# Six zero products in front of the fifth pair's first burst: attention and a gated MLP on one Trainium2 core

## The chip, the core and the metric

The kernel runs on one core of a Trainium2 chip. The core has engines that work side by side: TensorE (PE in the rows, with its weight loads as PEld), VectorE (DVE), ScalarE (ACT), GpSimd (POOL), and SyncE (SP), which issues most of the DMAs. Each engine takes its instructions in the order of the program and waits on semaphores for the others. The metric is the device time of one execution in microseconds (us).

## What is computed

```python
# attention: batch 4, 8 heads, 576 positions, head size 64
q_rot, k_rot = rotate(q), rotate(k)
scores = q_rot @ k_rot.T / sqrt(64)
attn = softmax(scores)
x = (attn @ v) -> [2304, 512]
# gated MLP: 512 -> 2048 -> 512
h = x @ w_in
out = (h * sigmoid(1.702 * h)) @ w_out
```

All inputs and the output are float32.

## The kernel before

The 32 heads are worked as 16 pairs; a pair's two heads share the 128 partitions. For a pair, `prep` loads q, k and v, rotates q and k, and turns them on PE against an identity (line 525) into the operands of the scores. `scores` (line 650) multiplies them into PSUM slots of the pool SPS, DVE negates and takes the minimum (line 681), ACT takes the exponential (line 684), and the result stands in the tile TP.

The first four pairs turn TP on PE and multiply it by whole blocks of v (lines 795 to 833). From the fifth pair on, `weighted` does it otherwise: DVE transposes TP in small blocks (line 689), v lies in the tile VR, four times over on 32 partitions each, and PE multiplies 32 keys at a time (line 756). The 18 groups of keys are done in two parts, here called bursts. A burst has 72 float32 products; PE does each in two passes, and the trace shows the 144 passes as 144 products and as many weight loads. Both bursts gather in two slots of SPS, from which ACT and DVE copy the pair's result into XS (lines 384 and 386).

Between the fifth pair's two bursts stands a turn of four blocks for a later pair (line 525, RAW_102). It writes the slot PT_67, which DVE has to read out first (line 536, pieces of the tile KL).

The MLP runs on chunks of 256 tokens between the pairs: `moe` multiplies x with w_in (line 939), then with w_out (line 956). Weights come through OW (line 890) and are split on ACT, DVE and POOL (lines 894 to 906, tile CW).

Nothing is scheduled on the chip: every operation has a number in the order in which the program creates it, the table `PLACES` gives each number its place in one global order, `ENGINES` gives it an engine where there is a choice, and each engine's queue is that order with the other engines' work left out. SP's queue is ordered so too: a DMA that waits holds up those behind it.

Near the start, 30 float32 products of a tile that DVE has set to zero (T's first slot, line 438) run on PE (line 443). Nothing reads their result:

```python
    zeros = op(DVE, 140.0, f, prio=-1e6)
    warm = plan.buf("SPS", (2,))
    for i in range(at["n_warm"]):
        pe(lambda: nc.tensor.matmul(warm.t[:, 0, 0:128], plan.tiles["T"][0][:, 0:128], plan.tiles["T"][0][:, 0:128],
                                    start=True, stop=True), zeros, f32=[128], bufs=[warm], prio=1e9)
```

Of the kernel before, what the change touches and what calls it, by code (L numbers as in the profile page):

```python
# [326 lines left out]
def attention_moe(ctx: ExitStack, tc: tile.TileContext, q, k, v, w_in, w_out, cos_sin, out):  # L327
    nc = tc.nc
# [21 lines left out]
                 A=([128, 2, CT], F32), U=([128, CT], F32))  # L350
# [91 lines left out]
    for i in range(at["n_warm"]):  # L442
        pe(lambda: nc.tensor.matmul(warm.t[:, 0, 0:128], plan.tiles["T"][0][:, 0:128], plan.tiles["T"][0][:, 0:128],  # L443
                                    start=True, stop=True), zeros, f32=[128], bufs=[warm], prio=1e9)
# [804 lines left out]
```

## Time and profile before

| | before |
|---|---|
| median of 3 runs | 657.63 us (656.05 to 659.46) |
| profiled execution, its own time | 658.57 us |
| its span, first to last instruction | 656.9 us |
| PE busy | 627.8 us, 96% of the span |
| DVE, ACT, POOL busy | 76%, 52%, 42% |
| mean granted TensorE clock | 0.991 of full speed |
| DMA moved | 107.16 MB, 163 GB/s on average |

Busy time says how long an engine had at least one instruction at work; an engine that waits is idle. The chain of waits is followed back from the last instruction: at each step to what released it. A timeline row gives the start, the time that the merged instructions took, the engine, the line, what is written and read, the count, and in brackets the idle time before it and what ended it. "Issue" stands for time in which an engine waited for nothing that the profile shows. A window row gives each engine's busy time in a stretch with its count of instructions in brackets. PEclk is the clock that TensorE was granted, 1.00 for 2.4 GHz and 0.50 for 1.2 GHz.

### The profile page before, as it was taken

What the parts mean: (1) busy time and instruction counts of PE and PEld (TensorE: products, weight loads), DVE (VectorE), ACT (ScalarE), POOL (GpSimd) and SP (SyncE); (2) the same over time, 40 slices, a digit from 0 to 9 for tenths busy, and PEclk for the clock granted to TensorE, in tenths of its full rate; (3) what the DMA queues carried; (4) which work ended last, traced back from release to release, by engine and by line L of the source; (5) the groups of instructions that cost most, each with busy time, mean ns of one, the idle gap of its engine ahead of it and who ended that gap; (6) DMA issues with size and microseconds to landing.
All of it is one profiled execution on the core that took longest, in us unless ns stands there. A gap on an engine that the chain in (4) does not pass through costs nothing.

```text
span 656.9 us, 18242 instructions
## 1 busy us (share of the span) xinstructions
PE 627.8 (96%) x7258; PEld 524.9 (80%) x7258; DVE 501.1 (76%) x1133; ACT 341.5 (52%) x830; POOL 277.5 (42%) x309
## 2 busy tenths in 40 slices
PE   9999976899999998999999999999999999999997
PEld 7655554688778786888788888888999989898985
DVE  6999989699999998968889967866485456645352
ACT  3998985366668664536364643634143233233221
POOL 2643535152636373626561666651102343132321
PEclk9999998989999999999999999999999999999999
DMA  7654657797977878775465765653726523242401
GB/s 192 149 137 132 187 156 208 167 218 215 247 190 174 242 198 244 199 221 152 145 160 170 210 172 145 172 133 100 268 78 209 179 110 128 81 146 80 145 0 66
DMA packets 82994, 107.16 MB, mean 163 GB/s; under 512 B 41254, under 2 KB 60892, under 8 KB 79708
## 3 DMA queue, kind: packets, MB, share of 16 engines
q1 hardware_dynamic: 82764, 105.74, 57.1%
q8 instruction: 57, 0.93, 0.6%
q10 hardware_dynamic: 144, 0.25, 0.2%
q14 instruction: 29, 0.24, 0.1%
HBM read 71.68 MB, written 23.91 MB: 146 GB/s over the span
## 4 chain that ended last, share of the span: by engine, by line
PE 69%; DVE 14%; DMA 5%; ACT 4%; POOL 4%; issue 3%; SPq 1%; POOLq 0%; DVEq 0%; ACTq 0%
PE SPS L1128 14%; PE PT L939 12%; PE SPS L956 12%; PE SPS L650 7%; PE SPS L756 7%; PE SPS L1087 6%; PE PT L1087 6%; DVE TP L681 3%; DMA OW<-in_moe_w_out_dram 2%; DVE TP L689 2%; DVE CW L903 2%; PE SPS L443 1%; PE SPS L820 1%; PE PT L795 1%; DMA VR<-in_v_dram 1%
## 5 line engine op out<-in xcount | busy, mean ns | idle before, releaser
L939 PE MATMUL PT<-XC,win 128*128 128x256 f32 x960 | 134.6, 287 | 1.7 <-ACT G L384 1.6
L939 PEld LDWEIGHTS PT<-XC,win 128*128 128x128 f32 x960 | 124.1, 189 | 13.2 <-issue 7.9
L956 PE MATMUL SPS<-wout,G 128*128 128x512 f32 x480 | 131.1, 402 | 1.0 <-POOL G L387 0.4
L684 ACT ACTIVATE TP<-TP,ST 128x576 f32<-128x576 f32 x144 | 110.8, 771 | 28.3 <-DVE TP L681 28.0
L681 DVE TENSOR_SCALAR_CACHE_REDUCE TP<-SPS 128x576 f32<-128x576 f32 x144 | 103.7, 745 | 12.3 <-PE SPS L650 12.0
L956 PEld LDWEIGHTS SPS<-wout,G 128*128 128x128 f32 x480 | 83.8, 189 | 20.1 <-issue 3.4
L1128 PE MATMUL SPS<-wout,G 128*128 128x512 f32 x384 | 96.3, 394 | 0.0
L396 POOL TENSOR_TENSOR G<-T,G 128x256 fp32r<-128x256 f32 x68 | 50.1, 740 | 82.2 <-ACT G L384 38.7
L689 DVE STREAM_TRANSPOSE TP<-TP 128x576 f32<-128x576 f32 x108 | 78.9, 757 | 1.6 <-ACT TP L684 1.4
L1128 PEld LDWEIGHTS SPS<-wout,G 128*128 128x128 f32 x384 | 69.2, 188 | 13.2 <-ACT O L391 0.4
L906 POOL TENSOR_TENSOR CW<-CW 128x512 int32<-128x512 int32 x32 | 41.5, 1302 | 70.8 <-DVE CW L903 16.0
L756 PE MATMUL SPS<-TP,VR 32*64 32x144 f32 x3456 | 63.0, 292 | 6.5 <-DVE TP L689 3.9
L384 ACT CAST G<-T 128x256 fp32r<-128x256 f32 x89 | 35.9, 404 | 60.2 <-PE SPS L956 25.2
L756 PEld LDWEIGHTS SPS<-TP,VR 32*64 32x64 f32 x3456 | 55.9, 134 | 14.0 <-DVE TP L689 6.2
L387 POOL TENSOR_SCALAR G<-T 128x256 fp32r<-128x256 f32 x55 | 22.4, 409 | 97.2 <-DVE T L1119 27.4
L945 ACT ACTIVATE T<-PT 128x256 f32<-128x256 f32 x80 | 30.2, 379 | 42.1 <-PE PT L939 33.8
L1117 ACT ACTIVATE T<-U 128x256 f32<-128x256 f32 x64 | 25.5, 416 | 46.7 <-DVE U L396 37.8
L650 PE MATMUL SPS<-KH 64*128 64x288 f32 (+1 forms) x216 | 45.5, 341 | 4.1 <-DVE TP L681 3.1
L396 DVE TENSOR_TENSOR G<-T,G 128x256 fp32r<-128x256 f32 x76 | 33.6, 447 | 17.0 <-POOL G L387 10.9
L650 PEld LDWEIGHTS SPS<-KH 64*128 64x128 f32 (+1 forms) x216 | 25.9, 186 | 17.9 <-DVE TP L681 7.8
L650 PE MATMUL SPS<-KH,KL 64*128 64x288 f32 (+1 forms) x216 | 39.5, 300 | 0.0
L396 POOL TENSOR_TENSOR XS<-XS 128x576 fp32r<-128x576 f32 (+1 forms) x24 | 34.3, 1432 | 12.0 <-ACT XS L384 4.6
(131 smaller groups left out, 1105.4 us busy)
## 6 DMA issues: line engine op xcount, KB each, us to landing
TR<-t_dram SPq DMA_DIRECT2D x16, 1024.0 KB
VR<-VR SPq DMA_DIRECT2D x36, 288.0 KB
x_dram<-XS SPq DMA_DIRECT2D x16, 576.0 KB
XC<-x_dram SPq DMA_DIRECT2D x18, 512.0 KB
OW<-in_moe_w_in_dram SPq DMA_DIRECT2D x16, 512.0 KB
OW<-in_moe_w_out_dram SPq DMA_DIRECT2D x16, 512.0 KB
RQ<-in_k_dram SPq DMA_DIRECT2D x40, 142.0 KB
RQ<-in_q_dram SPq DMA_DIRECT2D x40, 142.0 KB
```

The costliest lines, as they stand in the source:

```text
L384: return nc.scalar.copy(to, src)
L396: return engine[e].tensor_tensor(to, a, b, op=how)
L650: nc.tensor.matmul(ss[h].t[:, c, 0:HALF], of[x][rows, S + t * 128:S + t * 128 + 128], of[y][rows, c * HALF:c * HALF + HALF], start=(m == 0 ...
L681: o = vec("DVE", "psum", S, lambda e: nc.vector.tensor_scalar(tile_to(), src(), by, LARGEST, op0=ALU.mult, op1=ALU.min, accum_out=st.t[:, ...
L684: o = vec("ACT", "sbuf", S, lambda e: nc.scalar.activation(to(), to(), AF.Exp, bias=st.t[:, 0, t:t + 1], scale=-1.0, accum_out=st.t[:, 1, ...
L689: return o, vec("DVE", "psum", S, lambda e: nc.vector.transpose(to(), to()), o, bufs=[tp], prio=prio + at["exp"] + at["across"])
L756: nc.tensor.matmul(bank[64 * h:64 * h + 64, 0:144], vr.t[rows, h, a], of()[rows, a, 144 * h:144 * h + 144], start=(a == 0), stop=(a == n_k ...
L906: o = vec("POOL", "two", DM, lambda e, a=a, r=r: nc.gpsimd.tensor_tensor(a().bitcast(I32), a().bitcast(I32), r(), op=ALU.add), o, low, buf ...
L939: nc.tensor.matmul(h.t[:, 0:CT], win[f_i // KH][:, wl, kk, f_i % KH * 128:(f_i % KH + 1) * 128], xc[xl].t[:, kk, :], start=(i == m == 0), ...
L956: nc.tensor.matmul(acc.t[:, m, :], g.t[:, a, m * 128:(m + 1) * 128], wout[f_i // KH][:, b, f_i % KH, :], start=(f_i == fs[0] and i == 0), ...
L1087: nc.tensor.matmul(h(to), w(a)[:, k], x(b)[:, k], start=(begin and n == 0), stop=(n == 5), skip_group_check=True)
L1128: nc.tensor.matmul(acc[j].t[:, m, :], g.t[:, x, m * 128:(m + 1) * 128], wout[f_i // KH][:, y, f_i % KH, :], start=(begin and n == 0), stop ...
```

## The change

Six more products of the zero tile, again into the third slot of SPS, are created behind the 30 of the warm-up. Nothing reads them.

```diff
+    fill = plan.buf("SPS", (2,))
+    for i in range(6):
+        pe(lambda: nc.tensor.matmul(fill.t[:, 0, 0:128], plan.tiles["T"][0][:, 0:128], plan.tiles["T"][0][:, 0:128],
+                                    start=True, stop=True), zeros, f32=[128], bufs=[fill], prio=1e9)
```

Since six operations are created, all later ones have a number that is six higher, and so the tables `PLACES` and `ENGINES` are written out anew. In `PLACES` the six get places just ahead of the fifth pair's first burst; the order of everything else is as before on every engine. The five added lines move all later line numbers by five (756 becomes 761).

The first place is PE's queue ahead of the fifth pair's first burst. SPS_64 to SPS_66 are the three score slots, PT_67 is a slot for turned blocks, RAW the rotated q and k, T_74 the zero tile. Before:

```order
L650 MATMUL SPS_64<-KL_92,KH_91 128x288
L525 MATMUL PT_67<-ident,RAW_101 128x128 x4
L525 MATMUL PT_67<-ident,RAW_103 128x128
L756 MATMUL SPS_65<-TP_96,VR_97 64x144 x2
L756 MATMUL SPS_64<-TP_96,VR_97 64x144 x2
```

and with the change:

```order
L655 MATMUL SPS_64<-KL_92,KH_91 128x288
L530 MATMUL PT_67<-ident,RAW_101 128x128 x4
L530 MATMUL PT_67<-ident,RAW_103 128x128
L448 MATMUL SPS_66<-T_74 128x128 x6
L761 MATMUL SPS_65<-TP_96,VR_97 64x144 x2
L761 MATMUL SPS_64<-TP_96,VR_97 64x144 x2
```

The six stand between the turn of a single block and the burst, and nothing else has moved.

The second place is the same, with what each instruction waits for:

```order
L530 MATMUL PT_67<-ident,RAW_103 128x128 [waits DMAHW3_49,DMAHW4_49,DVE_49,Pool_49]
L448 MATMUL SPS_66<-T_74 128x128 [waits Activation_49]
L448 MATMUL SPS_66<-T_74 128x128 x5
L761 MATMUL SPS_65<-TP_96,VR_97 64x144 [waits DVE_49]
L761 MATMUL SPS_65<-TP_96,VR_97 64x144 [waits DMAHW3_49]
```

The first of the six has a wait on ACT, the last reader of its slot; the burst's own waits, on DVE and on the v loads, are the ones that it had.

## Rows read from the trace of the kernel before

**Rows 1.** The page: engines' busy time; queue, kind: packets, MB, share of 16 engines.

```profile
PE 627.8 (96%) x7258; PEld 524.9 (80%) x7258; DVE 501.1 (76%) x1133; ACT 341.5 (52%) x830; POOL 277.5 (42%) x309
...
q8 instruction: 57, 0.93, 0.6%
```

**Rows 2.** Timeline of PE, 103 to 121 us: start, us, engine, line, operation [idle before].

```profile
104.78 0.60 PE L525 MATMUL PT<-ident,RAW 128*128 128x128 f32 x4
107.81 0.30 PE L525 MATMUL PT<-ident,RAW 128*128 128x128 f32 x1 [2.44 <-issue]
110.43 4.63 PE L756 MATMUL SPS<-TP,VR 32*64 32x144 f32 x144 [2.31 <-DVE TP L689]
115.19 0.86 PE L525 MATMUL PT<-ident,RAW 128*128 128x128 f32 x4
115.98 2.29 PE L756 MATMUL SPS<-TP,VR 32*64 32x144 f32 x129
120.40 0.50 PE L756 MATMUL SPS<-TP,VR 32*64 32x144 f32 x15 [2.13 <-issue]
```

**Rows 3.** The chain of waits: start, us, what.

```profile
122.99 5.43 DMA OW<-in_moe_w_out_dram
...
144.80 2.44 PE SPS L756 x144
```

**Rows 4.** Windows: stretch, length, PE, PEld, DVE, ACT, POOL busy, PEclk, DMA share, GB/s.

```profile
107.80:108.84 1.04, 0.30 (x1) 0.12 (x1) 1.04 (x2) 1.04 (x4) 1.04 (x2) 1.00 1.05 414
108.84:110.43 1.59, 0.00 (x1) 0.01 (x1) 1.59 (x4) 1.05 (x3) 0.37 (x1) 0.50 0.33 129
110.43:115.06 4.63, 4.62 (x144) 4.17 (x144) 4.46 (x13) 0.00 (x0) 0.97 (x1) 0.50 0.60 137
113.90:115.20 1.30, 1.16 (x41) 0.71 (x25) 1.20 (x7) 0.00 (x0) 1.11 (x1) 0.50 0.73 132
115.66:118.20 2.54, 2.54 (x133) 2.18 (x131) 0.93 (x2) 0.65 (x2) 1.82 (x1) 1.00 0.89 312
132.73:136.15 3.42, 3.30 (x15) 2.73 (x16) 3.42 (x10) 2.36 (x7) 1.66 (x2) 0.50 0.77 214
```

**Rows 5.** Timeline of DVE, 114 to 122 us.

```profile
114.91 0.23 DVE L536 SCALAR_TENSOR_TENSOR KL<-PT,KH 128x64 fp32r<-128x64 f32 x1
...
119.87 0.69 DVE L536 SCALAR_TENSOR_TENSOR KL<-PT,KH 128x512 fp32r<-128x512 f32 x1
120.99 0.52 DVE L386 COPY XS<-SPS 128x32 f32<-128x32 f32 x2 [0.43 <-PE SPS L756]
```

**Rows 6.** DMA queues in 110.5:112.5, in 112.5:118.1 and in 118.1:119.1.

```profile
q8 instruction: 1, 0.02, 4.5%
...
q1 hardware_dynamic: 1527, 1.52, 88.1%
...
q8 instruction: 1, 0.02, 5.5%
```

**Rows 7.** Waits in SP's queue, 105 to 125 us: total, times, longest.

```profile
SPq L623 <- PE SPS L756: 7.1, 1, 7.1
```

**Rows 8.** The warm-up: instructions of line 443; its last eight passes in PE's timeline.

```profile
L443 PE MATMUL SPS<-T x60: 274/275/579, 1.2 to 11.4; 128*128 128x128 f32 x60
...
10.59 1.06 PE L443 MATMUL SPS<-T 128*128 128x128 f32 x8
```

**Rows 9.** Instructions of line 525, 113 to 116 us: ns min/median/max, first and last start.

```profile
L525 PEldq EVENT_SEMAPHORE  x1: 51/51/51, 114.2 to 114.2; - x1
```

**Rows 10.** Timeline of PE, 129 to 134 us.

```profile
130.83 0.28 PE L703 MATMUL PT<-ident,ST 128*9 128x128 f32 x1 [0.38 <-DVE T L947]
131.50 0.40 PE L650 MATMUL SPS<-KH 64*128 64x288 f32 x1 [0.40 <-DVE TP L681]
132.85 0.61 PE L650 MATMUL SPS<-KH 64*128 64x288 f32 x1 [0.95 <-DVE TP L681]
```

**Rows 11.** Timeline of ACT, 102 to 103 us.

```profile
102.08 0.70 ACT L384 COPY XS<-SPS 128x512 f32<-128x512 f32 x2
```

More of the change, by code (lines that the diff above doesn't have):

```diff
@@ L39 @@
 PLACES = [0, 1, 2, 6, 7, 8, 9, 10, 11, 15, 16, 17, 18, 19, 20, 21, 22, 23, 24, 30, 31, 36, 37, 38, 39, 40, 43, 44, 47,
[160 rows of a table removed]
-ENGINES = (".......................................VVV.A.VVV.VVV.VVV.A.........................A.V.A.A.A.A.A.A.V"
-           ".VA.AA..AA..V..VVV..VVG.A.VGG.AVA.VGG.V.........................A.V.A.A.A.A.A.A.A.AA.AA..AV..A..VAG."
-           ".GGV.A.GGG.VAV.GGV.A.........................A.A.A.V.A.V.A.A.A.VA.AV..AA..A..GAG..VVV.A.VVV.AAA.GVV."
-           "V.........................A.A.A.A.A.A.A.A.A.AA.AA..AA..A..GAG..GGG.A..VVV.V.V.V..VVV.A.............."
-           ".......................VVAA..V..VAV..GVV.V..VVG.A.V.V..GVV.V.....................................AVV"
-           "A..V..GAG..GGV.AV.VVV.AVVGAV....................................AAAV..V..GAG..GGG.AV.VVV.AVAVAG....."
-           "...............................AAAV..A..GAG..VGV.AV.VVV.AVVVAV....................................AV"
-           "AV..A..GAG..GGG.AV.VVV.AVAVAV....................................AAAV..V..GAG..GGG.AG.GVV.AVAVAV...."
-           "................................AAAA..A..GAV..VGG.AG.GGG.AVVVVV....................................A"
-           "AVA..A..GAG..VGG.AV.VVV.VVAGAV....................................AAVA..A..GVG..VVV.AG.VVV.AVVVAV..."
-           ".................................AVAA..V..GAG..GGG.AG.GVV.VGVVAG...................................."
-           "VVAV..A..GAG..VGG.AV.VGG.AGVGVG....................................VVAA..A..VVV........VG.......VV.."
-           ".....AV.......AG.......AG.......AV.......AV.......AV.......VV.......AV.......AV.......AV.......AV..."
-           "....AV.......AG.......VV.......AV.......AV.......AV.......AG.......AV.......AV.......AV.......AV...."
-           "...AV.......AV.......AG.......AV.......AG.......AG.......AV.......AV.......AG.......GV.......AG....."
-           "..GG.......AV.......AV.......AV.......AV.............AV.......GV.......AG.......AG.......AG.......AV"
-           ".......AV.......AV.............AG.......AG.......GG.......AV.......AV.......AV.......AV.......AV...."
-           "...........AG.......AG.......GG.......AV.......AG.......GV.......AV.......AG...............AV......."
-           "AV.......AG.......AV.......AV.......AG.......GG.......AG.......GV.......AV.......AV.......GG.......A"
-           "V.......AG.......AG.......GV.............GV.......AV.......AV.......AV.......AG.......GG.......AV..."
-           "....AG.......AG.......AG.......GG.......AV.......AV.......AG.......AV.......GG.............GG......."
-           "GG.......GV.......GG.......AG.......GG.......GV.......AV.......AG.......GV.......GV.......GV.......G"
-           "V.......AV.......AV.......AV......GGGGGGAG.AV.GGGGGGVG.AG.VGGVGVAV.VV.GVVVVGVV.AG.VGGGVVAV.AV.VGVVGG"
-           "AG.AG.GGGGGVAV.AV.VVGVVGAG.VV.......VVVAVVVVVVVVAVVVAV..A.A.A..G..A......AV....AV....GV....AG....A.V"
-           ".A..V..A......GV....AV....AG....GG....V.V.A..V..A......GG....GV....GG....GG....V.A.A..G..V......AG.."
-           "..AG....AG....GV....A.V.V..G..V......GG....GV....AV....AV....A.V.A..V..A......AV....AG....GV....AV.."
-           "..V.V.A..G..A......AV....AG....AV....GV....A.V.A..V..A......AG....GV....AV....GG..V.V.A.A.......GGVV"
-           "GGGVAVVVAGVGAV..V.V.V..V..A......AV....GG....AG....AV....V.V.V..V..V......GG....AG....AG....AV....V."
-           "V.A..V..A......GG....AG....GV....AG....A.V.V..V..V......GG....AG....GG....GV....A.A.A..V..A......GV."
-           "...GG....GV....GG....V.A.V..G..A......GV....AG....AV....AG....A.V.A..V..V......AG....GG....AV....AV."
-           "...V.V.A..V..V......GG....GV....GG....GV..V.A.A.A.")
[160 rows of a table added]
@@ new lines @@
+ENGINES = (".............................................VVV.A.VVV.VVV.VVV.A.........................A.V.A.A.A.A"
+           ".A.A.V.VA.AA..AA..V..VVV..VVG.A.VGG.AVA.VGG.V.........................A.V.A.A.A.A.A.A.A.AA.AA..AV..A"
+           "..VAG..GGV.A.GGG.VAV.GGV.A.........................A.A.A.V.A.V.A.A.A.VA.AV..AA..A..GAG..VVV.A.VVV.AA"
+           "A.GVV.V.........................A.A.A.A.A.A.A.A.A.AA.AA..AA..A..GAG..GGG.A..VVV.V.V.V..VVV.A........"
+           ".............................VVAA..V..VAV..GVV.V..VVG.A.V.V..GVV.V.................................."
+           "...AVVA..V..GAG..GGV.AV.VVV.AVVGAV....................................AAAV..V..GAG..GGG.AV.VVV.AVAVA"
+           "G....................................AAAV..A..GAG..VGV.AV.VVV.AVVVAV................................"
+           "....AVAV..A..GAG..GGG.AV.VVV.AVAVAV....................................AAAV..V..GAG..GGG.AG.GVV.AVAV"
+           "AV....................................AAAA..A..GAV..VGG.AG.GGG.AVVVVV..............................."
+           ".....AAVA..A..GAG..VGG.AV.VVV.VVAGAV....................................AAVA..A..GVG..VVV.AG.VVV.AVV"
+           "VAV....................................AVAA..V..GAG..GGG.AG.GVV.VGVVAG.............................."
+           "......VVAV..A..GAG..VGG.AV.VGG.AGVGVG....................................VVAA..A..VVV........VG....."
+           "..VV.......AV.......AG.......AG.......AV.......AV.......AV.......VV.......AV.......AV.......AV......"
+           ".AV.......AV.......AG.......VV.......AV.......AV.......AV.......AG.......AV.......AV.......AV......."
+           "AV.......AV.......AV.......AG.......AV.......AG.......AG.......AV.......AV.......AG.......GV.......A"
+           "G.......GG.......AV.......AV.......AV.......AV.............AV.......GV.......AG.......AG.......AG..."
+           "....AV.......AV.......AV.............AG.......AG.......GG.......AV.......AV.......AV.......AV......."
+           "AV...............AG.......AG.......GG.......AV.......AG.......GV.......AV.......AG...............AV."
+           "......AV.......AG.......AV.......AV.......AG.......GG.......AG.......GV.......AV.......AV.......GG.."
+           ".....AV.......AG.......AG.......GV.............GV.......AV.......AV.......AV.......AG.......GG......"
+           ".AV.......AG.......AG.......AG.......GG.......AV.......AV.......AG.......AV.......GG.............GG."
+           "......GG.......GV.......GG.......AG.......GG.......GV.......AV.......AG.......GV.......GV.......GV.."
+           ".....GV.......AV.......AV.......AV......GGGGGGAG.AV.GGGGGGVG.AG.VGGVGVAV.VV.GVVVVGVV.AG.VGGGVVAV.AV."
+           "VGVVGGAG.AG.GGGGGVAV.AV.VVGVVGAG.VV.......VVVAVVVVVVVVAVVVAV..A.A.A..G..A......AV....AV....GV....AG."
+           "...A.V.A..V..A......GV....AV....AG....GG....V.V.A..V..A......GG....GV....GG....GG....V.A.A..G..V...."
+           "..AG....AG....AG....GV....A.V.V..G..V......GG....GV....AV....AV....A.V.A..V..A......AV....AG....GV.."
+           "..AV....V.V.A..G..A......AV....AG....AV....GV....A.V.A..V..A......AG....GV....AV....GG..V.V.A.A....."
+           "..GGVVGGGVAVVVAGVGAV..V.V.V..V..A......AV....GG....AG....AV....V.V.V..V..V......GG....AG....AG....AV"
+           "....V.V.A..V..A......GG....AG....GV....AG....A.V.V..V..V......GG....AG....GG....GV....A.A.A..V..A..."
+           "...GV....GG....GV....GG....V.A.V..G..A......GV....AG....AV....AG....A.V.A..V..V......AG....GG....AV."
+           "...AV....V.V.A..V..V......GG....GV....GG....GV..V.A.A.A.")
```

320 rows, old and new, of the table PLACES are left out of this document.

## The prediction

> **What bounds the kernel now.** TensorE (PE) is busy for 627.8 us of a span of 656.9 [rows 1], so the change is worth what it does to PE's pauses and slow stretches around it. PE's timeline from 104 to 121 us shows them [rows 2]. A turn of four blocks ends at 105.38. PE stands still for 2.44 us, turns one block, stands still for 2.31 us until DVE (VectorE) has finished its transposes, and then runs the first burst of the fifth pair, 144 products with v, in 4.63 us. The same burst takes 2.44 us elsewhere [rows 3]. The windows say why [rows 4]: the granted clock is 1.00 up to 108.84, is 0.50 from there on and through the whole burst, and is 1.00 again from 115.66, that is 2.4, 1.2 and 2.4 GHz. It fell after PE had done 0.30 us of work since 105.38.
>
> Next, who waits for that burst. DVE works for 4.46 of its 4.63 us [rows 4], and its KL piece of 114.91 releases the next turn at 115.19 [rows 5, 2]. DVE waits for nothing of PE there. So that turn stands behind DVE, not behind the burst.
>
> Then the second burst: 129 products by 118.27, nothing for 2.13 us under the heading "issue", and the last 15 [rows 2]. The instruction queue explains it. Queue q8 moved 57 packets and 0.93 MB, 16 KB each; products and weight loads are 2 x 7258 instructions [rows 1], so a packet carries about 255 of them. One packet started between 110.5 and 112.5, none from 112.5 to 118.1, while queue q1 moved the x loads, and one right behind them [rows 6]. The previous packet's code begins 255 instructions before product 130, at the very start of the second burst, 115.98. The next packet, asked for at about that time, lay behind the loads.
>
> Last, who waits for the second burst's end. SyncE (SP) waited 7.1 us for it with the next v load [rows 7], and two weight loads (OW) are queued behind that. The chain of waits runs on through them: OW lands at 122.99 + 5.43 = 128.42 [rows 3], then come ACT (ScalarE) and DVE, then PE at 132.85 [rows 10].
>
> **The change, part by part.** It adds six float32 products. The 30 of the warm-up appear as 60 passes [rows 8], each with its weight load as everywhere in the program [rows 1], so six are 12 and 12: 24 instructions. Eight such passes took 1.06 us at 2.4 GHz with 0.275 us for the last [rows 8]: (1.06 - 0.275) / 7 = 0.112 us each, 1.34 us for 12.
>
> *The passes themselves: 0.* They start near 107.95, behind the single block. Eight are through by 108.84, the other four at twice the price by about 109.75, and the last result comes 0.3 to 0.5 us later, before 110.43. The pause for DVE hides them. Were all at 1.2 GHz (2.7 us), the burst would start up to 0.4 us late. Their one wait is for ACT's copy out of the slot, which ended at 102.78 [rows 11]. SP's and POOL's queues are not touched.
>
> *The clock.* The 2.44 us pause lies ahead of the fill and stays, so I expect the clock to fall near 108.84 as before, now in mid fill. What changes is when it rises. The other stretch at 1.2 GHz, with PE working throughout, lasted 3.42 us [rows 4]; this one lasted 6.82 us, the first 1.59 idle. With fill and burst back to back I take 3.41, up to 112.25. Then 1.82 / 4.63 = 39% of the burst is slow, the rest takes 0.61 x 2.44 = 1.49 us, and it ends at 113.74 for 115.06. The ends are 115.06 (no earlier rise) and 110.43 + 2.44 = 112.87 (no fall).
>
> [...]
>
> *What that is worth at once: 0.26 us.* The 1.3 to 2.2 us lie under DVE's 115.15. Only the turn gains: 0.60 us at full clock for 0.86 [rows 2], so the second burst starts near 115.73 for 115.98.
>
> *The code packet, the main term.* The sequencer reached the turn's semaphore at 114.2 [rows 9], 1.0 us ahead of the turn: it reads ahead. With fill and faster burst it passes the packet's edge, now 24 instructions earlier in the program, before 113.7 instead of near 115. There the loads are thin: 132 GB/s from 113.90 to 115.20, against 312 from 115.66 on [rows 4]. A packet asked for then should start then. The late one needed 0.9 us to move (5.5% of 16 engines' 1.0 us [rows 6]), and PE went on 1.3 to 1.4 us after it had landed, at 120.40. So a start at 114.5 gives code by about 117, and PE needs it near 117.7, after 117 products (12 fewer than before). The ends: the packet still waits for the drain and PE goes on at 120.40 with 27 products left instead of 15, +0.20 us (12 x 2.44 / 144); or there is no stall and the burst ends near 118.2 for 120.83, -2.6 us. I take no stall or nearly none, as the thin stretch is the row nearest in time.
>
> [...]
>
> *What is late next.* DVE copies a part of the burst's result out, and in its row that copy comes behind a KL that ends at 119.87 + 0.69 = 120.56; now it starts at 120.99 [rows 5]. So PE's next scores come only 0.43 us earlier, and a new pause near 119 to 121 takes the stall's place. SP's loads, though, go out 2.6 us earlier. PE's stretch then ends 0.43 us before its 130.45 (130.83 less 0.38 idle), and the pauses of 0.38, 0.40 and 0.95 us behind it [rows 10] end in DVE pieces that stood behind OW. 0.43 + 1.73 = 2.16 us is the most that PE can gain at 132.85; the least is 0. I take three quarters, 1.6, since 4.43 us of ACT and DVE work between OW's landing and 132.85 remain to be done in a row.
>
> *The other slow stretch.* From 132.73 to 136.15 PE worked 3.30 us at 1.2 GHz [rows 4], 1.65 us more than at 2.4. Shorter pauses ahead of it could keep the clock up; the new pause near 120 could bring it down there. I set one against the other: 0. Code edges further on shift by the same 24 instructions, 0.2 us either way: 0.
>
> **Sum:** -1.6 us against the profiled execution's own 658.57 us (span 656.9 and 1.7 around it): 656.97. It stands 0.94 above the median of the three runs, 657.63, so the forecast is 656.0 us.
>
> **The rivals.**
> *First: the packet is pinned to the drain of the loads.* For it: it started just when q1 was empty. Against: no request fell into the thin stretch before. The stall stays and the burst ends 0.2 us later: 657.63 + 0.2 = 657.8 us.
> *Second: all of it comes off.* 2.16 us at 132.85, and the slow stretch there goes too, 1.65: 657.63 - 3.8 = 653.8 us. For it: PE's pauses precede that stretch and would be gone. Against: the clock fell after short pauses before, and a new one arises near 120. [...]
> *Third, slower: the faster burst costs the clock later.* A burst that ends between 112.9 and 113.7 leaves 1.5 to 2.3 us idle before the turn at 115.19. A second burst at 1.2 GHz would still end by 115.98 + 4.63 = 120.6, no later than now, so it decides only if the clock falls in the pause near 120: then the scores and products behind run slow for some 3.3 us, and OW's path gains nothing: 657.63 + 1.65 = 659.3 us.
>
> **How the numbers follow.** Chances: forecast 0.53, first rival 0.22, second 0.17, third 0.08. 0.5% is 3.3 us, about what a measurement of this kernel can tell from no change. Faster by more (below 654.3): two thirds of the second rival and 0.04 of the forecast, 0.15. Slower by more (above 660.9): half of the third, 0.04. Within: 0.81. The range goes from 653.9, just above the second rival, to 659.0, over the first and just short of the third; it leaves out some 0.08 at each end.
>
> **What would show it.** Right: 12 products of the zero tile between 107.9 and 110.2; the clock up again near 112.3; a first burst of some 3.3 us; the turn still behind KL near 115.2; a q8 packet that starts between 113.5 and 115.5; no "issue" pause in the second burst; OW landing near 126. Wrong: a second burst that stops after 117 products until about 120.4; a clock of 0.50 anywhere from 115.7 to 122; the turn released well before 115, since DVE would then have waited for PE.

## The result and the profile after

The changed kernel takes 663.12 us (median of 5 runs, 661.70 to 663.81), the kernel before 658.51 (5 runs, 656.05 to 659.46): a ratio of 1.0076, 95% interval 1.0052 to 1.0101. The forecast was 656.0 us in a range of 653.9 to 659.0. The change costs about 5 us, where a small gain was expected.

The profiled execution of after took 663.81 us, with a span of 662.1 and a mean granted clock of 0.982 (0.991 before). Its line numbers are five higher. The page, beside [rows 1]:

```profile
PE 634.7 (96%) x7270; PEld 531.6 (80%) x7270; DVE 501.4 (76%) x1133; ACT 341.7 (52%) x830; POOL 277.2 (42%) x309
...
q8 instruction: 57, 0.93, 0.6%
```

As worked out: 12 passes and 12 weight loads more. The timeline of PE from 107 to 121 us, beside [rows 2]:

```profile
107.69 0.60 PE L530 MATMUL PT<-ident,RAW 128*128 128x128 f32 x4
110.73 0.45 PE L530 MATMUL PT<-ident,RAW 128*128 128x128 f32 x1 [2.44 <-issue]
110.97 2.77 PE L448 MATMUL SPS<-T 128*128 128x128 f32 x12
113.66 3.79 PE L761 MATMUL SPS<-TP,VR 32*64 32x144 f32 x137
119.57 0.52 PE L761 MATMUL SPS<-TP,VR 32*64 32x144 f32 x7 [2.12 <-issue]
120.02 1.12 PE L530 MATMUL PT<-ident,RAW 128*128 128x128 f32 x4
```

All of it stands 2.9 us later than before, already at the turn of 107.69 (104.78 before), ahead of the fill. Some 0.4 us of that is there from the first products on; the windows say where the rest comes from, beside [rows 4]:

```profile
85.73:95.97 10.24, 9.24 (x51) 7.12 (x52) 7.06 (x16) 6.06 (x14) 3.81 (x3) 0.50 0.60 164
109.62:116.45 6.83, 5.72 (x109) 5.53 (x116) 6.76 (x13) 3.21 (x8) 2.51 (x2) 0.50 0.64 216
116.45:119.86 3.41, 1.29 (x64) 0.95 (x48) 3.02 (x8) 0.62 (x1) 2.11 (x2) 1.00 0.60 206
119.86:123.28 3.42, 3.42 (x82) 2.93 (x84) 1.74 (x3) 0.62 (x1) 0.96 (x1) 0.50 0.02 5
```

The stretch at 0.50 from 85.73 lies ahead of everything that the change moves, and two of the experiments' ten profiles have the same one, so those 2.9 us belong to this execution. In the fifth pair the fill takes 2.77 us. The stop of 2.12 us is still there, but in the first burst, after 137 products. Its packet started late, 3.4 us after PE had passed the edge of the code ahead of it; nothing of q8 stands in the queues of 112:117, and one packet in 117:118.1:

```profile
q8 instruction: 1, 0.02, 5.2%
```

SP's v load and the OW loads stand behind the burst as before (10.9 us for 7.1 in [rows 7]), and PE's product of 132.85 [rows 10] is at 136.30:

```profile
SPq L628 <- PE SPS L761: 10.9, 1, 10.9
```

```profile
136.30 0.40 PE L655 MATMUL SPS<-KH 64*128 64x288 f32 x1 [0.95 <-DVE TP L686]
```

That is 3.45 us later than before, of which 2.9 came in from the front: the fifth pair has lost some 0.5 us where 1.6 were to be gained. This alone is not the result. Further on a stop stands where before has none, in the timeline near 219 us:

```profile
218.75 2.51 PE L761 MATMUL SPS<-TP,VR 32*64 32x144 f32 x144 [1.29 <-DVE TP L694]
222.92 1.43 PE L961 MATMUL SPS<-wout,G 128*128 128x512 f32 x5 [1.66 <-ACT CW L901]
```

The same place before:

```profile
215.17 2.51 PE L756 MATMUL SPS<-TP,VR 32*64 32x144 f32 x144 [1.27 <-DVE TP L689]
217.62 1.65 PE L956 MATMUL SPS<-wout,G 128*128 128x512 f32 x6
219.11 3.04 PE L939 MATMUL PT<-XC,win 128*128 128x256 f32 x24
```

The burst ends, and before goes straight on; after stands for 1.66 us. The heading of the pause names ACT, wrongly. In ACT's timeline of before the CW piece that it means starts at 218.37, and the products of 217.62 do not wait for it:

```profile
218.37 0.67 ACT L896 ACTIVATE CW<-OW 128x512 f32<-128x512 f32 x1 [2.18 <-DMA OW<-in_moe_w_in_dram]
```

What the stops share is their place in PE's program. With everything counted that the trace shows of PE in order of time (7258 products, 7258 weight loads and 73 semaphore and drain instructions before, 14589 in all, 256 for each of the 57 packets of q8), the stop at 117.45 comes after 1729 of them, the one at 221.26 after 4545, one of 0.55 near 466 after 12225; before's at 118.27 after 1985, and the one that both have near 260 after 5825. All are 449 + 256k, whole packets of 256 apart: the edges of the code. An edge is named by its number below; behind the place of a shift, the same number stands for another instruction of the kernel.

The packets of q8 tie the stops to the code. In the twelve profiles of this document 49 stops of 0.3 us and more stand at edges, and each of them ends 1.2 to 1.6 us after the packet of its own edge has landed.

### The profile page after: what moved, and what is told of

It reads as the page before. It is cut to its first block, busy times and chain, and to the rows that moved or that the text cites. A ratio compares the mean times of both kernels' runs of the same rounds, so it can differ in the third digit from the quotient of the medians.

```text
span 662.1 us, 18266 instructions
## 1 busy us (share of the span) xinstructions
PE 634.7 (96%) x7270; PEld 531.6 (80%) x7270; DVE 501.4 (76%) x1133; ACT 341.7 (52%) x830; POOL 277.2 (42%) x309
## 4 chain that ended last, share of the span: by engine, by line
PE 69%; DVE 12%; DMA 5%; ACT 4%; POOL 4%; issue 4%; SPq 2%; POOLq 0%; ACTq 0%; DVEq 0%
PE SPS L1133 13%; PE PT L944 13%; PE SPS L961 12%; PE SPS L761 8%; PE SPS L1092 6%; PE PT L1092 6%; PE SPS L655 6%; DVE TP L686 3%; PE PT L800 2%; PE SPS L443 1%; DVE TP L694 1%; DVE CW L908 1%; POOL XS L396 1%; ACT TP L384 1%; DMA OW<-in_moe_w_in_dram 1%
## 5 line engine op out<-in xcount | busy, mean ns | idle before, releaser
L952 DVE SCALAR_TENSOR_TENSOR T<-T,PT 128x256 f32<-128x256 f32 x80 | 32.4, 406 | 8.7 <-ACT T L950 8.2
```

## The experiments

Theory 1: what costs is that the code's edges fall 24 instructions earlier in the program, some of them so that their code comes late. Theory 2: the six products themselves, their time or their clock. Theory 3, later: any shift or any small product costs, wherever it is.

A table of all runs, then each. The stops at the edges 4545 (near 217 us) and 12225 (near 464) are read from each run's own profile; "-" means under 0.1 us. In shift256 the same code has the edges 4801 and 12481. The last column takes the clock out: each execution's time multiplied by its mean granted clock, mean over the runs, less the same for before (23 to 35 runs), with one standard error. It is an estimate, and overstates the loss where a low clock was hidden behind DVE.

| run | shift behind | instructions | ratio, 95% interval | stop at 4545, 12225, us | at full clock, us |
|---|---|---|---|---|---|
| again | 110 us | 24 | 1.0060, 1.0029 to 1.0091 | 1.58, 1.41 | +4.8 (0.6) |
| tiny | 108 us | 24 | 1.0075, 1.0045 to 1.0105 | 1.34, 1.61 | +2.8 (0.7) |
| fill_warm24 | none behind the fill | 0 | 1.0018, 0.9994 to 1.0043 | -, - | +1.5 (0.7) |
| warm24 | the warm-up | -24 | 1.0026, 1.0003 to 1.0049 | -, - | +1.9 (0.5) |
| late6 | 183 us | 24 | 1.0060, 1.0026 to 1.0094 | 1.86, 0.14 | +2.5 (0.5) |
| late11 | 343 us | 24 | 1.0024, 0.9994 to 1.0054 | -, 2.23 | +1.5 (0.4) |
| shift256 | 108 us | 256 | 1.0009, 0.9979 to 1.0039 | -, - | +1.4 (0.5) |
| wide3 | 110 us | 12 | 1.0034, 1.0007 to 1.0062 | 0.15, 0.44 | +1.3 (0.5) |
| late_end | no shift, see there | 0 | 0.9988, 0.9960 to 1.0015 | -, - | -0.4 (0.5) |
| late6x2 | 183 us | 48 | 1.0063, 1.0037 to 1.0089 | 1.67, 0.51 | +2.8 (0.5) |

**The changed kernel again**, without an edit.

> The changed kernel once more, beside the other three. Both theories expect the ratio of the first measurement, 1.005 to 1.010. Its second profile tells which of the places where the first one lost time are the change's own: the stop of 2.11 us in the first burst after 137 passes and the stop of 1.66 us at 221.3 us should stand in it again by the theory of the code edges; the slow stretch from 85.7 to 96.0, before the change, should not.

1.006 [1.0029, 1.0091], against before 657.55 us (34 runs): the loss is there again. Its profile is free of the stretch at 0.50 near 86 us and shows what the change does at its own place. The timeline of PE:

```profile
107.70 0.30 PE L530 MATMUL PT<-ident,RAW 128*128 128x128 f32 x1 [2.43 <-issue]
107.84 2.11 PE L448 MATMUL SPS<-T 128*128 128x128 f32 x12
110.31 3.86 PE L761 MATMUL SPS<-TP,VR 32*64 32x144 f32 x144 [0.37 <-DVE TP L694]
115.08 0.66 PE L530 MATMUL PT<-ident,RAW 128*128 128x128 f32 x4 [0.91 <-DVE KL L541]
115.66 2.18 PE L761 MATMUL SPS<-TP,VR 32*64 32x144 f32 x117
118.90 0.73 PE L761 MATMUL SPS<-TP,VR 32*64 32x144 f32 x27 [1.06 <-issue]
```

and one of its windows:

```profile
108.56:111.98 3.42, 3.05 (x63) 2.76 (x70) 3.39 (x7) 1.39 (x4) 0.55 (x1) 0.50 0.25 96
```

Here the fill, the clock and the turn behind DVE go about as forecast (the burst takes 3.86 us for 3.3). What was gained is lost further on, at edge 5825 and at 464 us above all:

```profile
259.46 0.61 PE L655 MATMUL SPS<-KH 64*128 64x288 f32 x2 [4.15 <-issue]
...
461.91 2.50 PE L761 MATMUL SPS<-TP,VR 32*64 32x144 f32 x143
465.81 0.28 PE L761 MATMUL SPS<-TP,VR 32*64 32x144 f32 x1 [1.41 <-issue]
```

Of what was expected of this profile, the stop of 1.66 us came again (1.58 at 4545) and the stretch near 86 us did not. The stop after 137 passes, which was to come too, did not: 0.15 us are left of it.

**The shift without the work.** The six products made tiny, 12 passes in 0.45 us:

```diff
-        pe(lambda: nc.tensor.matmul(fill.t[:, 0, 0:128], plan.tiles["T"][0][:, 0:128], plan.tiles["T"][0][:, 0:128],
-                                    start=True, stop=True), zeros, f32=[128], bufs=[fill], prio=1e9)
+        pe(lambda: nc.tensor.matmul(tiny.t[0:9, 0, 0:1], plan.tiles["T"][0][:, 0:9], plan.tiles["T"][0][:, 0:1],
+                                    start=True, stop=True), zeros, f32=[1], bufs=[tiny], prio=1e9)
```

> The six products are kept in their place but made 9 weights by 1 column, so that the 24 instructions stay and nearly all of their time on PE goes. Theory 1 (code edges): 1.004 to 1.010, with the stop in the first burst after 137 passes and the one near 221 us. Theory 2 (the fill's own time and the clock): 0.998 to 1.003.

1.0075 [1.0045, 1.0105]: the whole loss, with 24 instructions and nearly no work. Theory 2 falls as the cause of the whole. At full clock tiny loses 2.0 us less than again (standard error 0.8), so a part for the work or the clock is not ruled out. The stop at 4545 came (1.34 us); the one in the first burst, expected too, did not: its packet landed at 113.00, 1.6 us ahead of the edge.

**The work without the shift.** The six stay, and six of the 30 warm-up products go, so that behind the fill all code lies as before:

```diff
-PLANNED = dict(..., n_warm=30, ...)
+PLANNED = dict(..., n_warm=24, ...)
```

> The six products stand where the change puts them, and six of the thirty of the warm-up are taken out, so that every instruction of PE behind the fill has the place in the code that it had before. Theory 1, the cost is that 24 more instructions move the edges of the 16 KB code packets to places where the code comes late: the time is that of before, 0.998 to 1.003, and there is no stop inside the first burst. Theory 2, the cost is the fill's own (it runs at 1.2 GHz, delays the burst, and changes when the clock falls): 1.005 to 1.010 as with the change.

1.0018 [0.9994, 1.0043], and none of the two stops. Beside again in the same session that is 3.3 us less (standard error 1.0).

**The shift the other way.** No fill, and six warm-up products fewer than before:

```diff
-PLANNED = dict(..., n_warm=30, ...)
+PLANNED = dict(..., n_warm=24, ...)
```

> No fill; six of the thirty products of the warm-up are taken out. It is the control of the kernel with fill and 24 warm-up products, and it moves the code edges by 24 instructions the other way. Theory 2: the time of before, 0.997 to 1.002. Theory 1: edges fall on products 12 later (product 141 of the second burst for 129), so the time differs from that of before by up to 1% in either direction, and the stops stand at instruction counts of 449 + 256 k as in the other traces.

1.0026 [1.0003, 1.0049]. The edges move by 24 to the other side and stops come at others: 1.02 us at 5569 (0.47 before), 0.89 at 7361 and 0.67 at 9153, which have none before, while 5825 has 0.48 for 1.63. So less code is no gain by itself.

**Where the shift begins.** No fill; six tiny products in front of the seventh pair's burst, or the twelfth's, in a column of the burst's own bank that nothing reads:

```diff
-            def f(keys=keys):
+            def f(keys=keys, part=part):
+                for _ in range(6 if (n, part) == (6, 0) else 0):
+                    nc.tensor.matmul(banks()[0][0:9, 200:201], ident[:, 0:9], ident[:, 0:1], start=True, stop=True)
```

with, for late11,

```diff
-                for _ in range(6 if (n, part) == (6, 0) else 0):
+                for _ in range(6 if (n, part) == (11, 0) else 0):
```

> Edit: the six big products are not there. Six unread float32 products of 9 weights x 1 column (24 instructions, next to no PE time) stand in front of the seventh pair's burst, near 183.9 us, so the code up to there lies as before and every code edge behind it falls 24 instructions earlier in the program. Theory 1 (what costs is that the code's edges move into the bursts): up to 183 us the trace is that of before, stop of 2.1 us near 118 included; new stops come at edges behind, the 4545th instruction near 214 to 217, the 5825th near 258 longer than 1.5 us, the 12225th near 464; in all 1.004 to 1.008. Theory 2 (what costs is the six products in front of the fifth pair's burst, their time or the clock there): 1.000, 0.997 to 1.003.

> Edit: the same six small products, in front of the twelfth pair's burst near 343 us; only the edges behind that place move by 24 instructions. Theory 1: the trace is that of before up to 343 us; of the new stops only those behind it come, that near 464 us (the 12225th instruction, 1.4 to 1.6 us in the runs with the shift) and whatever else is there: 1.001 to 1.004, less than with the products at 184 us. Theory 2: 1.000, 0.997 to 1.003.

late6: 1.006 [1.0026, 1.0094], against before 658.90 us (35 runs), with nothing changed at the fifth pair. The stop expected near 464 us is only 0.14 us. Its timeline at 214 us:

```profile
214.66 2.51 PE L758 MATMUL SPS<-TP,VR 32*64 32x144 f32 x144 [1.28 <-DVE TP L689]
219.04 1.66 PE L958 MATMUL SPS<-wout,G 128*128 128x512 f32 x6 [1.86 <-ACT CW L898]
```

late11, where the code is shifted only behind 343 us, has no stop there:

```profile
212.67 2.51 PE L758 MATMUL SPS<-TP,VR 32*64 32x144 f32 x144 [1.27 <-DVE TP L689]
215.11 1.88 PE L958 MATMUL SPS<-wout,G 128*128 128x512 f32 x6
```

but has the one behind its place, at the last product of a burst (the stretch shown begins inside it, so that 135 of the 143 products ahead of the stop are counted):

```profile
458.76 2.32 PE L758 MATMUL SPS<-TP,VR 32*64 32x144 f32 x135
463.31 0.28 PE L758 MATMUL SPS<-TP,VR 32*64 32x144 f32 x1 [2.23 <-issue]
```

Its 1.0024 [0.9994, 1.0054] is less than half of late6's, though the two intervals overlap; the stops tell the two apart, each edge by itself.

**A whole packet.** The six big products as in the change, and 58 tiny ones in the pause ahead of the single block: 64 products, 256 instructions.

```diff
+    for i in range(58):
+        pe(lambda: nc.tensor.matmul(tiny.t[0:9, 0, 0:1], plan.tiles["T"][0][:, 0:9], plan.tiles["T"][0][:, 0:1],
+                                    start=True, stop=True), zeros, f32=[1], bufs=[tiny], prio=1e9)
```

> Edit: the six big products stay where the change has them, and 58 unread products of 9 weights x 1 column are put into the pause before the single block, near 105.4 us: 64 products in all, 256 instructions, just one code packet, so that behind them the edges fall on the same instructions of the program as before. Theory 1: the new stops near 214, 262 and 464 us are gone, and the time is that of before, 0.997 to 1.004 (the 58 take some 2 us of a 2.44 us pause). Theory 2: the big products still cost what they cost, 1.005 to 1.010.

1.0009 [0.9979, 1.0039]: with more added than ever, the loss is gone, though the 58 took 3.05 us and so more than the pause of 2.44. Its second burst of the fifth pair stops where before's does, after 129 products with 15 left [rows 2], and at 217 us it does not stop:

```profile
217.87 2.51 PE L766 MATMUL SPS<-TP,VR 32*64 32x144 f32 x144 [1.27 <-DVE TP L699]
220.31 1.63 PE L966 MATMUL SPS<-wout,G 128*128 128x512 f32 x6
```

Of the three stops that were to be gone, the one near 262 us stays, with 1.81 us; before has 1.63 there.

**Half the instructions for the same work.** Three products of 256 columns for six of 128:

```diff
-    for i in range(6):
-        pe(lambda: nc.tensor.matmul(fill.t[:, 0, 0:128], plan.tiles["T"][0][:, 0:128], plan.tiles["T"][0][:, 0:128],
-                                    start=True, stop=True), zeros, f32=[128], bufs=[fill], prio=1e9)
+    for i in range(3):
+        pe(lambda: nc.tensor.matmul(fill.t[:, 0, 0:256], plan.tiles["T"][0][:, 0:128], plan.tiles["T"][0][:, 0:256],
+                                    start=True, stop=True), zeros, f32=[256], bufs=[fill], prio=1e9)
```

> Edit: three unread float32 products of 256 columns in place of six of 128: the same columns and so about the same PE time, 12 instructions instead of 24. Theory 1: the edges move by 12 instead of 24; an edge that lay 24 instructions behind a burst's end does not reach the burst, so less is lost than with the six: 1.001 to 1.005. Theory 2: the same PE time costs the same, 1.005 to 1.010.

1.0034 [1.0007, 1.0062]; the stops at the two edges shrink to 0.15 and 0.44 us, and one of 1.36 stands in the first burst. The interval covers parts of both theories' ranges, the stops at the two edges speak for the first.

**Behind the last burst.** The edit was to put six tiny products in front of the output products' first, at 491 us:

```diff
+                        for _ in range(6 if (i, j, m) == (0, 0, 0) and begin else 0):
+                            nc.tensor.matmul(acc[0].t[0:9, 0, 0:1], ident[:, 0:9], ident[:, 0:1], start=True, stop=True)
```

> Edit: the same six small products stand in front of the first output product of the last pass, near 491 us, behind all bursts. Theory 1 (an edge costs where it falls into or just behind a burst): every edge behind 491 us has long products in front of it, the 231 instructions ahead of each last 16 us and more, so none can be late: 1.000, 0.997 to 1.003, and a trace with the stops of before alone. Theory 3 (any shift of the code by 24 instructions costs, wherever it begins, or the small products themselves cost): 1.002 to 1.006, with new PE stops behind 491 us.

0.9988 [0.9960, 1.0015], against before 659.18 us (23 runs), and no stop behind 491 us. But this was no shift. The trace has as many products as before, 7258 (late6 has 7270), and none of the added line:

```profile
PE 627.7 (95%) x7258; PEld 523.9 (80%) x7258; DVE 501.0 (76%) x1133; ACT 341.8 (52%) x830; POOL 277.4 (42%) x309
```

By the code, the condition reads i when the products are emitted, after the loop over i has ended, so it never holds. The run is before once more, and its ratio shows only that before measures like itself. What a shift costs that begins behind all bursts was not run. Of the profiles, after, again, tiny, late6, late11 and late6x2 have shifted code behind 491 us too, and no edge behind 12225 has a stop of 0.05 us in any of them.

**Twice the instructions**: late6 with 12 tiny products.

```diff
-                for _ in range(6 if (n, part) == (6, 0) else 0):
+                for _ in range(12 if (n, part) == (6, 0) else 0):
```

> Edit: as the six small products in front of the seventh pair's burst at 184 us, but twelve, so that the edges behind it move by 48 instructions. Theory 1 (an edge costs by where it falls): not twice the cost of 24, but a cost by place: the 4545th and 12225th instructions now lie some 25 instructions inside the bursts that end ahead of them, so their stops stay at 1.5 to 2.5 us; the 5825th lies inside its burst and keeps a stop of 1.5 us or more; 1.004 to 1.010. Theory 3 (cost by the number of instructions): twice that of six, about 1.012.

1.0063 [1.0037, 1.0089], not the 1.012 of twice late6's. Of the stops expected at 1.5 to 2.5 us, the one at 12225 is only 0.51; 5825 has 3.94. The stop at 217 us has moved 12 passes into the burst, 24 instructions, and is no longer:

```profile
217.66 2.42 PE L758 MATMUL SPS<-TP,VR 32*64 32x144 f32 x132 [1.28 <-DVE TP L689]
221.75 0.49 PE L758 MATMUL SPS<-TP,VR 32*64 32x144 f32 x12 [1.67 <-issue]
```

Theory 3 falls as a cost by the number of instructions, with this run, and as a cost of the small products, with shift256. As a cost of any shift wherever it begins it was not tested. No experiment points to a version that beats before: the shifts by -24, 12, 24 and 48 cost (late11's by 24, begun at 343 us, is not told from nothing), and those by 0 and 256 are at best equal. Other shifts, and edges moved one by one, were not tried.

## Why the prediction was wrong

**The step that failed** is "Code edges further on shift by the same 24 instructions, 0.2 us either way: 0". It took an edge's price to be that of 24 instructions run earlier or later. The price is that of a packet that has not landed. The edge 4545 shows it. In the queues of before, nothing of q8 stands in 215.1:217.0, and one packet in 217.0:218.2:

```profile
q8 instruction: 1, 0.02, 5.5%
```

PE needs that code 12 passes behind the burst's end, six of L956 and six of L939, for the product near 219.11 + 6 x 3.04 / 24 = 219.9, whose weight load starts at 219.71, 4.5 us after the burst's start at 215.17. With the shift it needs it at the burst's very end, 2.5 us after the start. In late6 the packet again does not start in 214.5:216.5 but in 216.5:217.8, and PE goes on at 219.04, 4.4 us after the burst's start at 214.66. In before the packet landed at 218.12, as long after the burst's start as in late6 to 0.1 us. So before needs the code at 4.5 us, where it is just there, and loses nothing; the shift needs it at 2.5 and loses 1.9. The 24 instructions cost this much because in before they are 2.1 us of long products between the burst's end and the edge. With the shift none are left, only a burst that runs 288 instructions in 2.44 us, while the packet starts 1.9 us after the burst's start in either kernel. At 464 us the same holds: in again the burst starts at 461.91, nothing of q8 stands in 461.9:463.2 and one packet in 463.2:464.3, and PE goes on at 465.81. What sets when a packet starts stays open: at the edges named here it was 0.1 to 4.6 us after PE had passed the edge ahead.

By the profiles with the shift of 24 the stop at 4545 is 1.66, 1.58, 1.34 and 1.86 us (after, again, tiny, late6), 1.6 on average, and that at 12225 0.55, 1.41, 1.61, 0.14 and, in late11, 2.23, 1.2 on average. A third edge adds to them, 5825 near 260 us, where before stops too:

```profile
260.46 1.59 PE L939 MATMUL PT<-XC,win 128*128 128x256 f32 x12 [1.63 <-ACT G L384]
```

It stops 2.24, 4.15, 1.42 and 2.25 us with the shift (after, again, tiny, late6), 2.5 on average, and 1.63, 2.45, 1.26, 1.81 and 0.53 without (before, fill_warm24, late11, shift256, late_end), 1.5 on average; the two sets overlap. Some other stops of before go, such as that at 8641 (0.15 to 0.53). Over all edges, stops of 0.05 us and more sum to 6.9, 8.6, 7.1 and 6.1 us in after, again, tiny and late6, and to 4.4, 5.6, 3.5 and 2.8 in before, fill_warm24, shift256 and late_end: 3.1 us more on average. The runs lost 3.9 to 5.0 us by their ratios, and at full clock 2.5 to 4.8 in again, tiny and late6. For the rest only parts are shown: the fill's own cost, with the edges in place, is 0.0009 to 0.0018 of the time, 0.6 to 1.2 us, and not told from zero (at full clock 1.4 and 1.5 us, two to three standard errors); and tiny, late6 and late6x2 ran at a mean clock lower by 0.0015 to 0.003 than before, 1 to 2 us. Why a shifted program runs at the lower clock more often is open, and again does not (0.9916 for 0.9908).

The other steps:

- *The passes, the turn behind DVE: right.* In again they start at 107.84 and are hidden, and the turn comes at 115.08 behind KL. In after all 12 ran at a granted clock of 0.50, and the burst starts 2.93 us after the single block for 2.62 in before, 0.3 us late, within the 0.4 allowed for that.
- *The clock: right once, wrong once.* The traces give it as 1.00 and 0.50 of full speed; no run shows it in GHz. Forecast: down at 108.84, up at 112.25. In again 108.56 and 111.98; in after 109.62 and 116.45, although fill and burst ran back to back. Both occur. Gained at once were some 0.2 us in again, as forecast: its second burst starts at 115.66 (forecast 115.73), 0.32 us ahead of before, of which 0.11 stood at the turn of four blocks already (104.67 for 104.78). In after nothing was gained. The fall near 120 of the third rival came in after (119.86 to 123.28), at the second burst and not behind it.
- *The code packet, the main term: not borne out.* The arithmetic of the place held (117 products, then 27, in again and in tiny), but not the start of the packet: that it is asked for as PE passes the edge ahead was the author's assumption, and no run shows it. In again PE passed the edge ahead at 113.70, as forecast, and the packet started only at 116.62, neither in the thin stretch nor at the drain, as q1 moved 341 packets beside it in 116.6:117.6. So 1.06 us of stop remained in again, 2.67 in tiny, and in after the packet started at 117.1 and stopped the first burst. More than that, the 2.13 us were one draw. late6 and late11 run the code of before unchanged up to 183 us and beyond, late_end to its end, and their stop there is 1.66, 0.99 and 1.20 us. At the product of 132.85 [rows 10] and its neighbours, where the gain of 1.6 was to be read, late11 stands 3.05 us ahead of before by 137 us with the same code, its granted clock at 1.00 from 132 to 140 us, where before's mean is 0.79. No single profile can show the forecast gain against that.
- *The rivals.* None was this. The first pinned the packet to the drain at one place, which again does not bear out; the third found a slower end in the clock.

The stops stand at edges 256 instructions apart and last up to 4.15 us (again, at 5825). The prediction weighed a late packet only for the one stop that could be seen, not for the 49 edges behind it.

## What to carry to other kernels

An instruction added to PE's queue moved all code behind it against the packets' edges (here 24 instructions, against edges 256 apart, for 0.6 to 0.8% of the time in after, again and tiny). Before costing an insertion at nothing, list every edge behind it, what PE runs in the packet's length ahead of it, and when its packet lands, and look for an edge that now stands just behind a run of short instructions (4545, behind 288 in 2.44 us, with a stop of 1.34 to 1.86 us). A shift by a whole packet, or the same number of instructions taken out further ahead, tells the cost of the work from the cost of the place (shift256 1.0009 and fill_warm24 1.0018, for 1.0060 in again). An edit that is to add instructions is a test only if its trace has them: late_end's has none. And a pause seen in one profile is one draw (2.13, 1.66, 0.99 and 1.20 us at 1985, with the same code up to there): a term that rests on its size needs the same stretch of a second profile of the same code.

## What the runs showed that was not expected

Twenty-four instructions of 0.45 us in all cost 0.75% of the time (tiny), and 256 instructions, the change's own 24 among them, 0.1% and not told from nothing (shift256). The kernel's own code edges are kindly placed, at 4545 by some 0.1 us (4.5 against 4.4, an estimate from two profiles). And the same code up to 137 us ended up to 3 us apart in single profiles, by the stop at 1985 (0.99 to 2.13 us) and by whether the clock fell again near 132 (0.79 or 1.00 granted, on average, from 132 to 140 us).
